# Global filter and gated feed-forward on one core: four PSUM banks and a new place for the filter copies in the first sequence

## The chip, the cores and the metric

The kernel runs on one core of one Trainium2 chip. The metric is the device time in microseconds (us) of one execution. The core has five engines that run their own instruction streams and meet at semaphores: PE (TensorE, matrix products into PSUM), DVE (VectorE), ACT (ScalarE), POOL (GpSimd) and SP (SyncE, which here only issues DMAs). POOL issues DMAs too.

## The reference

`x` is 8 sequences of 3008 tokens by 256 features. A filter acts in the frequency domain, and its output goes into a gated feed-forward block:

```python
X = np.fft.rfft(x, axis=1)
Y = X * (filt_r + 1j * filt_i)[None, :, :]
y = np.fft.irfft(Y, n=x.shape[1], axis=1).reshape(-1, 256)
rms = np.sqrt(np.mean(y * y, axis=-1, keepdims=True) + 1e-06)
xn = y / rms * rms_g
g = xn @ w_gate                       # 256 -> 1536
out = (g / (1 + exp(-g)) * (xn @ w_val)) @ w_out
```

## The kernel before

3008 is 47 x 64, so each transform is two small dense products with tables of sines and cosines, with a multiplication by the filter between the forward and the inverse one. The sequences are numbered `b` = 0 to 7. For `b` = 1 to 7 the mixing steps are laid by a plan (`at(slot, ...)`) between the feed-forward steps of the sequence before: one slot per block of 128 hidden features (`gv`, the gate and value products, and `down`, the output product), 576 slots in all. The instructions stand in the order in which the program writes them; no scheduler moves them.

Nothing can cover the mixing of sequence 0, so it stands alone ahead of slot 0. This first part is what the change touches. It keeps the data in SBUF, where later sequences go through HBM. In order of the program:

- **Set-up.** `x_load` (L180, eight DMAs on POOL's queue), clearing of half of each filter tile (POOL L613 and L614, DVE L620, ACT L610), and `f_load` (L464): real filters `fr[c]` on SP's queue, imaginary filters `fi[c]` on POOL's queue, for four chunks `c` of 8 frequencies. Behind the last `fi` chunk POOL issues `w_load(0)`, the first third of the three weight matrices.
- **Tables.** `wi_group(g)` (L556), g = 0 to 7, transposes a group of tables on PE into PSUM (`pst`); DVE copies one half out and ACT the other. Both halves take fixed PSUM banks, `bank(0)` and `bank(3)`. Groups 0 to 3 run ahead of `at_unit`, groups 4 to 7 between its calls. `warm_up(n)` (L575) is n products of zeros into a scratch bank.
- **Forward transform.** `at_unit(m, dh)` (L489) makes `aT`; one half is copied by DVE, the other by ACT. `at_unit` m reads columns 4m to 4m+3 of `x`, six columns to a chunk. `t1_unit(g)` (L501), g = 0 to 7, transposes `aT` (`pt`), in two PSUM banks that alternate; DVE copies the even ones and ACT the odd ones. `b_unit(0, i)` (L228), i = 0 to 15, is the second product (`psb`), two frequencies each, in four banks.
- **Filter.** Each filter tile is needed in both halves of the partitions. `f_dup(c)` (L475) copies 64 partitions to the other 64: chunk 0 by DVE (L478) and ACT (L485), the real part of chunks 1 and 2 by ACT (L480), all others by POOL (L482, L487). Calls stand ahead of i = 0, 3, 7 and 11. `b_unit` i uses chunk i/4. Its two products (L262, L263) run on DVE straight from PSUM, except for i = 1, 4, 7, 10, where ACT first copies the PSUM tile to `v` (L260) and POOL multiplies.
- **Inverse transform.** `bit_unit(i)` (L521) makes `pgt`, copied to `gT` (L538, L536) by ACT and once by DVE. Pairs of them stand behind `b_unit` i = 5, 7, ... with a lag of five, four behind the loop.
- **To the first feed-forward block.** `t2_unit` (L540) transposes `gT`. `n_first` (L361) is the last product, of which ACT takes the square `sq` and DVE the scaled `y`. `q_unit(0, 0)` sums the squares on PE (`psq`), DVE makes `u`, POOL takes the power -0.5 (`rho`, L347), `scale_split` halves it into two fp16 numbers `hl`, `warm_up(6)` follows, `scale_apply` spreads `hl` over the partitions on PE (`psr`), and DVE makes `xn`. Then slot 0 starts with `gv`.

`w_load(1)` and `w_load(2)` are issued by POOL behind `b_unit` i = 11. `bank(i)` (L192) names the six PSUM places that all these steps share: `mx`, `pg` (two buffers), `pv` (two buffers), `mb`, `po1`, `po0`.

Of the kernel before, what the change touches and what calls it, by code (L numbers as in the profile page):

```python
# [11 lines left out]
FP16 = mybir.dt.float16  # L12
AXT = mybir.ActivationFunctionType
ALU = mybir.AluOpType
# [6 lines left out]
P = 128  # L21
D = 256
# [7 lines left out]
HALF = 64  # L30
# [92 lines left out]
def kernel(  # L123
# [11 lines left out]
    nc = tc.nc  # L135
# [35 lines left out]
    gsb = glob.tile([P, 2], FP32)  # L171
# [20 lines left out]
    def bank(i, name):  # L192

        pool, tag = ((psM, "mx"), (psG, "pg"), (psV, "pv"), (psB, "mb"), (psO, "po1"), (psO, "po0"))[i]
        return pool.tile([P, 512], FP32, tag=tag, name=name)
# [32 lines left out]
    def b_unit(b, i):  # L228
        if b:
            ps = bank(3, "psb")  # L230
        else:
            ps = bank((0, 3, 4, 5)[i % 4], "psb")
        ps = ps.rearrange("p (a d) -> p a d", a=2)
        for u in range(2):
            k = 2 * i + u
            if b:
                w, t = late_p["wb"], st[b]["t2"][k // KC][:, k % KC, :]
            else:
                w, t = wbp, st[0]["t2"][k // 4][:, k % 4, :]
            nc.tensor.matmul(ps[:, u, :], w[:, k, :], t, start=True, stop=True)  # L240
        f1, f2 = filt(2 * i, 2)
        if b:
            s1 = late_p["sp"].tile([P, 2, D], FP16, tag="s1", name="s1")
            s2 = late_p["sp"].tile([P, 2, D], FP16, tag="s2", name="s2")
            if b > 1:
                nc.vector.tensor_tensor(out=s1, in0=ps, in1=f1, op=ALU.mult)  # L246
                st[b]["s"][i] = (s1, s2, ps, f2)
                return
        elif i % 2:
            s1 = hp.tile([P, 512], FP16, tag="sg", name="sg").rearrange("p (a d) -> p a d", a=2)  # L250
            s2 = hhs[(i // 2) % 4].rearrange("p (a d) -> p a d", a=2)
        else:
            ss = xnp.tile([P, 2, 512], FP16, tag="xn", name="ss")
            s1, s2 = (ss[:, e, :].rearrange("p (a d) -> p a d", a=2) for e in range(2))
        eng = nc.vector
        if (i % 3 == 1) if b else (i in (1, 4, 7, 10)):
            eng = nc.gpsimd
            v = yp.tile([P, 2, 512], FP32, tag="y", name="v")
            v = v[:, 0, :].rearrange("p (a d) -> p a d", a=2)
            nc.scalar.activation(out=v, in_=ps, func=AXT.Copy)  # L260
            ps = v
        eng.tensor_tensor(out=s1, in0=ps, in1=f1, op=ALU.mult)  # L262
        eng.tensor_tensor(out=s2, in0=ps, in1=f2, op=ALU.mult)  # L263
        st[b]["s"][i] = (s1, s2)
# [96 lines left out]
    def n_first():  # L361

        y = yp.tile([P, 2, 512], FP32, tag="y", name="y")
        sq = sqp.tile([P, 2, 512], FP16, tag="sq", name="sq")
        for dh in range(2):
            ps = bank(1 + dh, "psn")
            for q in range(4):
                nc.tensor.matmul(ps[:, ts(q, P)], st[0]["t4"][0][:, q, ds(dh * P, P)], wai2,
                                 start=True, stop=True)
            nc.scalar.activation(out=sq[:, dh, :], in_=ps, func=AXT.Square)  # L370
            nc.vector.tensor_scalar(out=y[:, dh, :], in0=ps, scalar1=gsb[:, dh:dh + 1], scalar2=None,
                                    op0=ALU.mult)
        st[0]["sq"][0] = sq
        st[0]["y"][0] = y

# [88 lines left out]
    def f_load(c, src, t, p0, eng):  # L464
        lo = 1 if c == 0 else 0
        eng.dma_start(t[p0 + 16:p0 + 63:2, :, :].rearrange("p a d -> p (a d)"),
                      raw(src, c * KC, [[64 * D, 24], [1, KC * D]]))
        for g in range(2):
            eng.dma_start(t[p0 + 1 + 24 * g:p0 + 24 + 24 * g:2, lo:KC, :],
                          raw(src, 64 * (1 + 11 * g) - c * KC - lo,  # L470
                              [[64 * D, 12], [-D, KC - lo], [1, D]]))
        if c == 0:
            eng.dma_start(t[p0 + 1:p0 + 48:2, 0, :], raw(src, 32, [[64 * D, 24], [1, D]]))

    def f_dup(c):  # L475
        a, e = fr[c][HALF:P], fr[c][0:HALF]
        if c == 0:
            nc.vector.tensor_copy(out=a, in_=e)  # L478
        elif c < 3:
            nc.scalar.activation(out=a, in_=e, func=AXT.Copy)  # L480
        else:
            nc.gpsimd.tensor_copy(out=a, in_=e)  # L482
        a, e = fi[c][0:HALF], fi[c][HALF:P]
        if c == 0:
            nc.scalar.activation(out=a, in_=e, func=AXT.Copy)  # L485
        else:
            nc.gpsimd.tensor_copy(out=a, in_=e)  # L487

    def at_unit(m, dh):  # L489
        ps = bank(1 + dh, "pat")  # L490
# [10 lines left out]
    def t1_unit(g):  # L501
        if g < 6:
            if g % 2 == 0:
                st[0]["t2t"] = t2p.tile([KR, KC, D], FP16, tag="t2", name="t2")
            dst = st[0]["t2t"][:, 4 * (g % 2):4 * (g % 2) + 4, :]
        else:
            dst = t3p.tile([KR, 4, D], FP16, tag="t3", name="t2")
        st[0]["t2"][g] = dst
        ps = psO.tile([P, 4, D], FP16, tag="po%d" % (g % 2), name="pt1")
        af = aT.rearrange("p a k -> p (a k)")  # L510
        for a in range(4):
            for dh in range(2):
                b0 = dh * H * P
                src = af[:, b0:b0 + 32 * P].rearrange("p (i k) -> p k i", k=K2)[:, 4 * g + a, :]
                nc.tensor.transpose(ps[:, a, ts(dh, P)], src, ident)
        if g % 2 == 0:
            nc.vector.tensor_copy(out=dst, in_=ps[0:KR])
        else:
            nc.scalar.activation(out=dst, in_=ps[0:KR], func=AXT.Copy)
# [36 lines left out]
    def wi_group(g):  # L556

        lo = 1 if g == 0 else 0
        for e in range(2):
            ps = bank(3 * e, "pst").rearrange("p (a d) -> p a d", a=4)  # L560
            for a in range(lo, 4):
                w = wbp[:, 4 * g + a, :]
                if e:
                    for p0 in (0, HALF):
                        nc.tensor.matmul(ps[p0:p0 + HALF, a, :], w[:, HALF - p0:P - p0], pm,
                                         start=True, stop=True)
                else:
                    nc.tensor.matmul(ps[:, a, :], w, pm, start=True, stop=True)
            dst = wi[:, e, 4 * g + lo:4 * g + 4, :]
            if e:  # L570
                nc.scalar.activation(out=dst, in_=ps[:, lo:4, :], func=AXT.Copy, scale=sgn)
            else:
                nc.vector.tensor_copy(out=dst, in_=ps[:, lo:4, :])

    def warm_up(n):  # L575
        pw = bank(4, "pw")
        for i in range(n):
            nc.tensor.matmul(pw, wz[:, 0:P], wz, start=True, stop=True)

# [5 lines left out]
    def w_load(q):  # L585
        cols = ts(q, DFF // 3)
        for src, dst in ((moe_w_gate, wg), (moe_w_val, wv)):
            nc.gpsimd.dma_start(dst[:, :, cols], src.rearrange("(dt p) j -> p dt j", p=P)[:, :, cols])
        nc.gpsimd.dma_start(wo[:, ts(q, JT // 3), :],
                            moe_w_out.rearrange("(jt p) d -> p jt d", p=P)[:, ts(q, JT // 3), :])  # L590

    with tc.manual_schedule():
# [28 lines left out]
            zero(fi[c][HALF:P])  # L621
        for c in range(4):
            f_load(c, filt_r, fr[c], 0, nc.sync)
            f_load(c, filt_i, fi[c], HALF, nc.gpsimd)
        w_load(0)
        with nc.allow_non_contiguous_dma(reason="one gain a partition"):
            nc.sync.dma_start(gsb, moe_rms_g.rearrange("(a p) -> p a", p=P))

        warm_up(16)
        for g in range(4):  # L630
            wi_group(g)
        warm_up(4)
        for m in range(6):
            for dh in range(2):
                at_unit(m, dh)
            if m < 4:
                wi_group(m + 4)
                warm_up(2)
        for i in range(8):
            t1_unit(i)  # L640
        f_dup(0)
        for i in range(16):
            if i % 4 == 3 and i < 15:
                f_dup(i // 4 + 1)
            b_unit(0, i)
            if i % 2 and i >= 5:
                bit_unit(i - 5)
                bit_unit(i - 4)
            if i == 11:
                w_load(1)  # L650
                w_load(2)
        for i in range(12, 16):
            bit_unit(i)
        t2_unit(0, 1)
        t2_unit(1, 0)
        n_first()
        t2_unit(2, 1)
        t2_unit(3, 0)
        q_unit(0, 0)
        t2_unit(4, 1)  # L660
        t2_unit(5, 0)
        scale_split(0)
        warm_up(6)
        scale_apply(0, 1)
        for c in range(NXC):
            x_load(1, c)
# [122 lines left out]
```

## Time and profile before

| | us |
|---|---|
| median of 15 runs | 952.79 (951.13 to 957.91) |
| profiled execution, its own time | 952.95 |
| its span, first to last instruction | 951.1 |

So 1.85 us of the profiled execution lie outside its span. Over the whole span PE is busy for 899.3 us (95%), DVE for 666.7 (70%), ACT for 632.5 (66%) and POOL for 391.6 (41%).

The first part, by stages of the span (busy us of each engine, PE's granted clock as a share of full speed):

| stage, us | what runs | PE | DVE | ACT | POOL | clock |
|---|---|---|---|---|---|---|
| 0 to 20.9 | tables, `at_unit` | 17.27 | 15.07 | 15.86 | 15.58 | 1.00 |
| 20.9 to 28.5 | `t1_unit` | 5.39 | 4.24 | 4.10 | 2.62 | 1.00 |

A busy time counts overlapped instructions once. In lines of the timeline, the first number is the start and the second the length in us, then come engine, line and operation, what is written and read, how many instructions are merged, and in brackets the idle time of the engine just before and what ended it.

### The profile page before, as it was taken

The page shows a single profiled execution, that of the slowest core. Times are in us where ns is not written, and L with a number is a line of the kernel's source. Part 1 is how long each engine was busy: PE and PEld are TensorE (multiplying, and loading weights), DVE is VectorE, ACT ScalarE, POOL GpSimd, SP SyncE. Part 2 cuts the span into 40 slices and gives each one's busy share as a digit, 9 for nine tenths or more (in the row PEclk, how much of TensorE's full clock was granted, in tenths as well). Part 3 has the DMA queues.
Part 4 walks back from the last instruction along what each step waited for, and adds up shares of the span by engine and source line. Part 5 has one row for each costly group of instructions (what it writes and reads, how often), then busy time and mean ns, then how long its engine had stood idle before and what let it go on. Part 6 is the DMA issues. An engine that isn't in the chain of part 4 may idle for free.

```text
span 951.1 us, 17799 instructions
## 1 busy us (share of the span) xinstructions
PE 899.3 (95%) x6339; PEld 565.0 (59%) x6339; DVE 666.7 (70%) x1051; ACT 632.5 (66%) x1066; POOL 391.6 (41%) x316
## 2 busy tenths in 40 slices
PE   8669788989999999999999999999999999999997
PEld 5546455555556666566666666666666666666654
DVE  6544445677778878788768788688868888555554
ACT  7647567577757776687757776687757775576543
POOL 7742269444532554145522554135522554033200
PEclk9779899999999999999999999999999999999999
DMA  9483655843466535743565435733353223322211
GB/s 200 75 132 82 173 117 112 208 101 85 109 138 131 122 74 103 182 101 90 117 147 125 123 73 109 178 80 79 98 143 94 78 64 65 108 62 57 52 27 45
DMA packets 87509, 101.21 MB, mean 106 GB/s; under 512 B 15984, under 2 KB 64048, under 8 KB 87036
## 3 DMA queue, kind: packets, MB, share of 16 engines
q1 hardware_dynamic: 78476, 83.82, 35.5%
q0 software_dynamic: 8944, 16.26, 10.9%
q8 instruction: 50, 0.82, 0.4%
q14 instruction: 39, 0.32, 0.1%
HBM read 67.93 MB, written 46.79 MB: 121 GB/s over the span
## 4 chain that ended last, share of the span: by engine, by line
PE 72%; DVE 8%; DMA 7%; POOL 5%; issue 4%; ACT 3%; SPq 0%; POOLq 0%; DVEq 0%; ACTq 0%
PE po L437 21%; PE pg L420 21%; PE pv L420 20%; DVE hh L425 3%; DMA t<-g_tmp 3%; PE psi L285 3%; PE psb L240 2%; PE psn L320 2%; PE psa L204 2%; DVE o L443 1%; ACT sg L424 1%; POOL s L276 1%; DMA g_tmp<-t 1%; DVE s L273 1%; DMA rb<-r_tmp 1%
## 5 line engine op out<-in xcount | busy, mean ns | idle before, releaser
L425 DVE TENSOR_TENSOR hh<-pv,sg 128x512 f16<-128x512 f32 (+1 forms) x576 | 391.9, 680 | 234.4 <-ACT sg L424 119.2
L424 ACT ACTIVATE sg<-pg 128x512 f16<-128x512 f32 (+1 forms) x576 | 338.9, 588 | 243.4 <-PE pg L420 235.4
L437 PE MATMUL po<-wo,hh 128*128 128x256 f16 x2256 | 344.0, 273 | 1.9
L420 PE MATMUL pg<-xn,wg 128*128 128x512 f16 (+1 forms) x1152 | 338.4, 375 | 1.0 <-DVE xn L393 1.0
L420 PE MATMUL pv<-xn,wv 128*128 128x512 f16 (+1 forms) x1152 | 338.4, 375 | 0.0
L437 PEld LDWEIGHTS <-hh 128*128 128x128 f16 x2256 | 216.6, 98 | 110.4 <-issue 11.2
L276 POOL TENSOR_TENSOR s<-s,s 128x512 f16<-128x512 f16 x96 | 110.7, 1153 | 352.9 <-DVE s L273 297.7
L420 PEld LDWEIGHTS <-wv 128*128 128x128 f16 x1152 | 112.7, 98 | 132.0 <-issue 1.6
L404 POOL TENSOR_TENSOR xn<-y,rb 128x1024 f16<-128x1024 f32 (+1 forms) x46 | 129.0, 2804 | 64.2 <-DMA rb<-r_tmp 56.9
L273 DVE TENSOR_TENSOR s<-psb,fi 64x512 f16<-64x512 f32 x192 | 132.3, 689 | 5.9
L420 PEld LDWEIGHTS <-wg 128*128 128x128 f16 x1152 | 109.1, 98 | 13.9 <-issue 1.7
L290 ACT ACTIVATE t<-psi 96x512 f16<-96x512 f32 x112 | 66.4, 593 | 20.8 <-PE psi L285 16.6
L347 POOL TENSOR_TENSOR rho<-u,mhalf 128x4 f32<-128x4 f32 (+1 forms) x48 | 48.5, 1011 | 64.0 <-DVE u L345 63.6
L326 ACT ACTIVATE y<-psn,gsb 128x512 f32<-128x512 f32 (+1 forms) x94 | 63.8, 679 | 9.9 <-PE psn L320 2.0
L246 DVE TENSOR_TENSOR s<-psb,fr 128x512 f16<-128x512 f32 x96 | 65.5, 682 | 4.1 <-PE psb L240 3.5
L206 ACT ACTIVATE t<-psa 128x512 f16<-128x512 f32 x84 | 50.2, 597 | 11.4 <-PE psa L204 7.9
L285 PE MATMUL psi<-s,wi 128*128 128x256 f16 x248 | 45.5, 272 | 10.7 <-POOL s L276 5.7
L332 ACT ACTIVATE sq<-psn 128x512 f16<-128x512 f32 (+1 forms) x94 | 54.7, 582 | 0.0
L240 PE MATMUL psb<-t,wb 96*128 96x256 f16 x224 | 43.1, 273 | 4.1 <-DMA t<-z_tmp 4.1
L285 PEld LDWEIGHTS <-wi 128*128 128x128 f16 x248 | 24.1, 97 | 38.4 <-issue 13.9
L320 PEld LDWEIGHTS <-t 128*128 128x128 f16 x368 | 28.4, 98 | 23.3 <-issue 3.1
L320 PE MATMUL psn<-tb,t 128*128 128x128 f16 x368 | 35.9, 219 | 2.4 <-ACT sq L332 1.0
(96 smaller groups left out, 482.5 us busy)
## 6 DMA issues: line engine op xcount, KB each, us to landing
out_dram<-o SPq DMA_DIRECT2D x84, 256.0 KB
xc<-in_x_dram POOLq DMA_DIRECT2D x56, 192.0 KB, 5.7
rb<-r_tmp SPq DMA_DIRECT2D x42, 256.0 KB
z_tmp<-t SPq DMA_DIRECT2D x112, 96.0 KB
t<-z_tmp SPq DMA_DIRECT2D x28, 384.0 KB
g_tmp<-t SPq DMA_DIRECT2D x56, 192.0 KB
t<-g_tmp SPq DMA_DIRECT2D x92, 96.0 KB
out_dram<-o SPq DMA_DIRECT2D x12, 192.0 KB
```

Of the source, the lines that this page charges most:

```text
L246: nc.vector.tensor_tensor(out=s1, in0=ps, in1=f1, op=ALU.mult)
L273: nc.vector.tensor_tensor(out=s2[a], in0=ps[e], in1=f2[e], op=ALU.mult)
L276: nc.gpsimd.tensor_tensor(out=s, in0=s1, in1=s2, op=ALU.add)
L285: nc.tensor.matmul(ps[:, u, :], wi_at(q, 2 * i + u), ss[q][:, u, :], start=(q == 0), stop=(q == n - 1))
L290: nc.scalar.activation(out=st[b]["t3"][c][:, 2 * r:2 * r + 2, :], in_=ps[0:KR], func=AXT.Copy)
L320: nc.tensor.matmul(ps[:, ts(q, P)], st[b]["t4"][n1p // XC][:, n1p % XC, ds(dh * P, P)], wai if b else wai2, start=True, stop=True)
L326: nc.scalar.activation(out=y[:, dh, 0:w], in_=ps[:, 0:w], func=AXT.Identity, scale=gsb[:, dh:dh + 1])
L404: nc.gpsimd.tensor_tensor(out=xv, in0=yv, in1=rv.unsqueeze(1).to_broadcast([P, 2, n, P]), op=ALU.mult)
L420: nc.tensor.matmul(ps[:, 0:w], wt[:, dt_, ts(jt, P)], xn[:, dt_, 0:w], start=(dt_ == 0), stop=(dt_ == 1))
L424: nc.scalar.activation(out=sg[:, 0:w], in_=pg[:, 0:w], func=AXT.Silu)
L425: nc.vector.tensor_tensor(out=hh[:, 0:w], in0=pv[:, 0:w], in1=sg[:, 0:w], op=ALU.mult)
L437: nc.tensor.matmul(po[s4 // 2][:, s4 % 2, :], hh[:, ts(s4, P)], wo[:, jt, :], start=(jt == 0 and s4 % 2 == 0), stop=(jt == JT - 1 and (s4 ...
```

## The change

Four things change, all of them in the first part:

1. `wi_group` and `t1_unit` each take four PSUM banks in turn instead of two. The copy of `t1_unit` 7 goes from ACT to DVE. Groups 4 and 5 stand together behind `at_unit` 0, groups 6 and 7 behind 1 and 2. The calls of `warm_up` there are left out but the first, which has 14 products instead of 16.
2. `f_dup` copies chunks 0 and 1 on POOL, chunk 2 on ACT, and of chunk 3 the real part on ACT and the imaginary part on POOL. On POOL's queue the copies of chunk 0 now stand behind the DMAs of `fi` chunk 2, then the DMAs of `fi` chunk 3, then the copies of chunk 1, then `w_load(0)`. The copies of chunk 2 stand ahead of `b_unit` i = 4, those of chunk 3 ahead of i = 9.
3. The four products that POOL makes are those of i = 2, 5, 8, 11 instead of 1, 4, 7, 10.
4. In `n_first` ACT makes the first half of `y`, behind both squares. The six warm-up products ahead of `psr` become two behind the first two `t2_unit`, three behind the next two, and four ahead of `scale_split`, all in bank `mx`.

```diff
-        if (i % 3 == 1) if b else (i in (1, 4, 7, 10)):
+        if (i % 3 == 1) if b else (i in (2, 5, 8, 11)):
...
-            nc.vector.tensor_scalar(out=y[:, dh, :], in0=ps, scalar1=gsb[:, dh:dh + 1], scalar2=None,
-                                    op0=ALU.mult)
+            if dh:
+                nc.vector.tensor_scalar(out=y[:, dh, :], in0=ps, scalar1=gsb[:, dh:dh + 1], scalar2=None,
+                                        op0=ALU.mult)
+            else:
+                y0, p0 = y[:, dh, :], ps
+        nc.scalar.activation(out=y0, in_=p0, func=AXT.Identity, scale=gsb[:, 0:1])
...
     def f_dup(c):
-        a, e = fr[c][HALF:P], fr[c][0:HALF]
-        if c == 0:
-            nc.vector.tensor_copy(out=a, in_=e)
-        elif c < 3:
-            nc.scalar.activation(out=a, in_=e, func=AXT.Copy)
-        else:
-            nc.gpsimd.tensor_copy(out=a, in_=e)
-        a, e = fi[c][0:HALF], fi[c][HALF:P]
-        if c == 0:
-            nc.scalar.activation(out=a, in_=e, func=AXT.Copy)
-        else:
-            nc.gpsimd.tensor_copy(out=a, in_=e)
+        for t, a, e in ((fr[c], HALF, 0), (fi[c], 0, HALF)):
+            if c == 2 or (c == 3 and a):
+                nc.scalar.activation(out=t[a:a + HALF], in_=t[e:e + HALF], func=AXT.Copy)
+            else:
+                nc.gpsimd.tensor_copy(out=t[a:a + HALF], in_=t[e:e + HALF])
...
-        ps = psO.tile([P, 4, D], FP16, tag="po%d" % (g % 2), name="pt1")
+        pool, tag = ((psO, "po0"), (psO, "po1"), (psM, "mx"), (psB, "mb"))[g % 4]
+        ps = pool.tile([P, 4, D], FP16, tag=tag, name="pt1")
...
-        if g % 2 == 0:
+        if g % 2 == 0 or g == 7:
...
-            ps = bank(3 * e, "pst").rearrange("p (a d) -> p a d", a=4)
+            ps = bank((0, 3, 4, 5)[(2 * g + e) % 4], "pst").rearrange("p (a d) -> p a d", a=4)
...
-    def warm_up(n):
-        pw = bank(4, "pw")
+    def warm_up(n, bk):
+        pw = bank(bk, "pw")
...
             f_load(c, filt_r, fr[c], 0, nc.sync)
-            f_load(c, filt_i, fi[c], HALF, nc.gpsimd)
-        w_load(0)
+            if c < 3:
+                f_load(c, filt_i, fi[c], HALF, nc.gpsimd)
...
-        warm_up(16)
+        warm_up(14, 1)
         for g in range(4):
             wi_group(g)
-        warm_up(4)
         for m in range(6):
             for dh in range(2):
                 at_unit(m, dh)
-            if m < 4:
-                wi_group(m + 4)
-                warm_up(2)
+            for g in ((4, 5), (6,), (7,), (), (), ())[m]:
+                wi_group(g)
         for i in range(8):
             t1_unit(i)
         f_dup(0)
+        f_load(3, filt_i, fi[3], HALF, nc.gpsimd)
+        f_dup(1)
+        w_load(0)
         for i in range(16):
-            if i % 4 == 3 and i < 15:
-                f_dup(i // 4 + 1)
+            if i == 4:
+                f_dup(2)
+            if i == 9:
+                f_dup(3)
             b_unit(0, i)
...
         t2_unit(1, 0)
+        warm_up(2, 0)
         n_first()
         t2_unit(2, 1)
         t2_unit(3, 0)
+        warm_up(3, 0)
         q_unit(0, 0)
         t2_unit(4, 1)
         t2_unit(5, 0)
+        warm_up(4, 0)
         scale_split(0)
-        warm_up(6)
         scale_apply(0, 1)
```

## The prediction

> **What bounds the kernel now.** First the table of stages:
>
> ```profile
> 28.50:54.40 25.90, 16.35 (x157) 12.75 (x156) 15.04 (x25) 14.35 (x22) 21.81 (x18) 0.67 0.37 56
> 54.40:65.80 11.40, 8.48 (x56) 5.56 (x57) 4.44 (x11) 2.88 (x5) 5.52 (x10) 0.56 0.94 141
> 120.00:951.00 831.00, 805.27 (x5583) 504.00 (x5580) 603.92 (x947) 560.30 (x956) 332.10 (x241) 1.00 0.44 103
> ```
>
> (Columns: stage, length, busy PE, PE weight loads, DVE, ACT, POOL, clock, DMA.) From 120 us on PE is busy 97%, and the change leaves that part alone. All of the change lies ahead of 65.8 us. There PE waits for others, and in the filter stage POOL is the busiest (84%). Next the chain of waits, from 45 us to the first complete gate product at 65.79:
>
> ```profile
> 45.04 1.86 POOL fr L482
> ...
> 46.96 1.90 POOL fi L487
> ...
> 49.50 0.68 DVE sg L262
> ...
> 54.39 1.22 PE pt L549 x8
> ...
> 57.34 1.41 DVE y L371 x2
> ...
> 60.84 2.72 PE pw L578 x6
> 63.56 0.87 PE psr L389 x8
> ```
>
> POOL's last two copies end last; DVE then makes its remaining seven products, 0.60 us apart, to 53.18; PE and ACT finish `gT` by 54.34. The rest is a row of short steps, one of them six warm-up products at half clock (0.453 us each). DVE's timeline says who is late, and POOL's why:
>
> ```profile
> 46.94 0.69 DVE L262 TENSOR_TENSOR ss<-psb,fr 128x512 f16<-128x512 f32 x1 [3.89 <-POOL fr L482]
> 48.89 0.69 DVE L263 TENSOR_TENSOR ss<-psb,fi 128x512 f16<-128x512 f32 x1 [1.26 <-POOL fi L487]
> ```
>
> ```profile
> 25.12 0.76 POOL L589 DMA_DIRECT2D wo<-in_moe_w_out_dram  x1 [0.42 <-DMA fi<-in_filt_i_dram]
> 30.95 1.27 POOL L262 TENSOR_TENSOR sg<-v,fr 128x512 f16<-128x512 f32 x1 [5.07 <-ACT v L260]
> 32.19 1.26 POOL L263 TENSOR_TENSOR hh<-v,fi 128x512 f16<-128x512 f32 x1
> 33.52 1.89 POOL L487 COPY fi<-fi 64x2048 f32<-64x2048 f32 x1
> ```
>
> POOL waits 5.07 us until 30.95 and then works without a gap to 48.85: four pairs of products (2.5 us each) and four copies (1.89 each). In `t1_unit` the wait is for banks, as PE's timeline shows:
>
> ```profile
> 24.96 1.19 PE L515 MATMUL pt<-tb,aT 128*128 128x128 f16 x16 [0.50 <-ACT t L519]
> 26.73 0.67 PE L515 MATMUL pt<-tb,aT 128*128 128x128 f16 x8 [0.58 <-ACT t L519]
> ```
>
> **The banks.** Today table groups come 1.16 us apart, each half waiting for its bank. With four banks DVE's copies follow at 0.60, so group 3 is copied at 10.5 instead of 12.2, and a warm-up of 0.97 us goes. Ten copies (four tables, six `aT`) by 0.60 to 0.69 on each of DVE and ACT then run to about 17.2. The last chunk of `x` lands at 15.24 by the trace's landing records, which leaves this nearly as it is. `aT` is complete at 17.25 instead of 20.87. The eight `t1_unit` take 0.66 us of PE each, with no wait for a bank (bank 0 is read by 18.8 and needed at 20.1). PE is done at 22.7 and DVE's last two copies at 23.4, instead of 28.45: **5.0 us earlier**. This alone is no gain; what counts is who is last behind it.
>
> **POOL's new row.** Landing records: `fr` chunk 0 at 18.40, `fi` 0 at 19.04, `fr` 1 at 22.89, `fi` 1 at 23.68, `fr` 2 at 28.98, `fi` 2 at 26.28, `fi` 3 at 29.33, `fr` 3 at 31.95. POOL has issued `fi` 2 by 18.3. Then two copies to 22.3, three DMA issues (0.55 + 0.6 + 0.6) to 24.1, two copies to 27.9, three weight issues (0.76 + 0.72 + 0.76) to 30.2. Moving `fi` 3 past two copies costs nothing: its issue ends at 24.1 while the queue is busy with `fi` 2 until 26.28, and it is read only at 38.5. `w_load(0)` is issued 4.3 to 6.4 us later and landed 9 us after its issue today; slot 0 needs it at 55. The pair of i = 2 runs from 30.2 to 32.7. The pair of i = 5 needs `v` from ACT, which now sits behind the copies of chunk 2: ACT waits for `fr` 2 from 24.4 to 28.98 and then copies to 32.8 (1.91 each), `v` at 33.4. So i = 5 runs to 35.95, i = 8 to 38.5, the copy of `fi` 3 to **40.4**, i = 11 to 42.9. Queued behind ACT's two copies are `gT` copies and the next `v`; PE has two buffers for `pgt`, and `v` of i = 8 is made at 35.9, when POOL wants it.
>
> DVE makes i = 0, 1, 3 (23.4 to 27.0), waits for `fi` 1 (27.9), makes 4, 6, 7 to 31.0, and 9 and 10 by 38.4. The first product of i = 12 is made by 39.9, the second waits for 40.4, and seven products by 0.60 end at **44.6 instead of 53.18**: 8.5 us. POOL's last pair, 42.9, is done by then; PE has four pairs left of 0.35 us at full clock or 0.65 at half. DVE loses a copy (1.22) and a `y` (0.7).
>
> POOL's copies read while DVE reads PSUM. POOL's product takes 1.27 us beside DVE in the rows above, so I add nothing for sharing.
>
> **The tail.** From the last product to `pt` 1.21 us as today: 45.8. At half clock, with today's durations: eight `pt` 1.22, two warm-ups 0.91 (beside ACT's copy 0.6, so 0.3 on the path), `psn` 0.85, `pt` 0.85, three warm-ups 1.36, `psq` 0.35, `u` 0.2, `rho` 1.05 and `hl` 0.4 (beside them `pt` and four warm-ups, 2.65, which end last by 0.95), `psr` 0.9, `xn` 1.3: the first complete gate product at 56.25, 9.5 us earlier than 65.79. At full clock the warm-ups hide, and `sq`, `u`, `rho` and `hl` are the path: 52.7, 13.1 us earlier. The row of this stage says 0.56 of full speed, so I lie nearer the half-clock end: 10.5. `y` on ACT behind both squares ends ahead of `psr` in both sums.
>
> Sum: 952.95 - 10.5 = 942.45; against the median (0.16 lower) **942.3**. Behind slot 0 everything shifts together: weights 2 and 3 are issued from 42.9, landed 11 us after the first issue today, and slot 4 needs them at 60.
>
> **Two rules weighed.** The program has a library reload for POOL right ahead of its first product, in both kernels. The Trainium skill (GPSIMD Engine Reference, Instruction dispatch) says that the first call of a freshly loaded routine pays about 6 us for code, with no instruction to be seen. The row: POOL's 5.07 us idle ends 0.09 after `v`, so a cost of up to 5 could be hidden there, and 6 could not. Today's 5 us cover is gone in the new order (`v` is made at 25). The row gives 0 to 5.07, the rule 6. I take 0, since copies and products in the same row follow each other without a gap. The other: TensorE: Matmul & The Clock Gate (The HAM clock gate) states that PE's clock halves after idle windows and needs some 3.4 us of steady work to come back. The row: half clock from 50.8 to 64.45, full just as slot 0 starts, behind 3.6 us of unbroken warm-ups and `psr`. The new warm-ups are spread; by the rule slot 0 may start at half clock. PE is only 75% busy in the first 10 us of slots, so one window of 3.4 us there costs 1 us or so. By the row I add nothing, by the rule 1 us; it stays in the range.
>
> **Rivals.** (1) The reload is exposed: POOL is 5.1 to 6 us later, less 0.75 that i = 5 waits anyway; the products end at 49 to 49.8, and with the shorter tail the time is 947 to 948. Chance 0.17. (2) The denser row keeps PE at full clock in the tail: 939 to 940. For it, the new row has 2 us less idle between bursts; against it, waits for POOL at 30 and 40 us. 0.13. (3) **Slower**: slot 0 starts at half clock and stays there. A PE-bound slot loses half its time, so the 10.5 us are eaten from 21 us of half clock on; at 25 us the time is 955. Against it, the chip raised the clock after one full window wherever the trace is dense, and the slots are. 0.05. (4) The change does nothing, because landings set the pace: `fr` 2 at 28.98 is late for ACT. The sum has this wait and it costs 0.75; if landings moved by 8 us it would be true, within 0.2% of before. 0.03. The forecast itself, 940 to 945: 0.62.
>
> The 80% range is 938.3 to 948, from full clock to an exposed reload. About 0.2% (2 us) is what can be told from no change: faster 0.93, same 0.02, slower 0.05.
>
> **What would show it.** Right: `t1_unit` without waits for banks, done near 23.4; POOL's copies from 18.5; POOL's first product near 30.2; DVE's last near 44.6; the first complete gate product at 53 to 56. A gap on POOL between the third weight issue and its first product is the reload. The forecast is wrong if POOL's copies are stretched well over 1.9 us, or if the gain at the first gate product is not found at the end.

## The result and the profile after

| | before | changed |
|---|---|---|
| median, us | 953.26 (949.92 to 957.91, 47 runs) | 939.88 (939.06 to 943.28, 9 runs) |
| profiled execution, us | 952.95 | 943.11 |
| its span, us | 951.1 | 941.3 |

The ratio of the times is 0.9866, 95% interval [0.9851, 0.9881]: the changed kernel is 12.8 us faster (11.3 to 14.2). The forecast was 942.3, a gain of 10.5.

The stages of the changed kernel, cut where the same steps end (`t1_unit` copied, `gT` complete, first complete gate product; the columns are those of the stage table in the prediction):

```profile
25.90:46.00 20.10, 12.58 (x158) 10.00 (x158) 15.14 (x26) 13.94 (x22) 19.76 (x19) 0.87 0.54 83
46.00:55.00 9.00, 7.85 (x58) 5.17 (x59) 3.89 (x10) 3.34 (x6) 4.68 (x8) 0.72 1.16 168
110.00:941.00 831.00, 805.00 (x5568) 503.36 (x5565) 602.08 (x945) 558.61 (x954) 331.62 (x240) 1.00 0.44 102
```

Up to the end of `t1_unit` 2.5 us are gone. The filter stage is 20.1 us long instead of 25.9, and POOL is busy in 98% of it: it is still who is last, with nothing left between its instructions. The tail is 9.0 us instead of 11.4. The last row is as dense as before (805.00 us of 831, before 805.27), so in this pair of executions the gain lies ahead of slot 0. The end of the same stretch in the chain of waits (start, length in us, what):

```profile
39.16 1.17 POOL fi L484
...
40.41 1.26 POOL sg L262
41.67 1.23 POOL hh L263
...
46.00 1.20 PE pt L547 x8
47.20 0.85 PE pw L576 x2
48.06 0.85 PE psn L368 x8
48.91 0.85 PE pt L547 x8
49.77 1.28 PE pw L576 x3
51.05 0.20 PE psq L341 x8
...
55.04 0.38 PE pg L424
```

POOL again leads, through the copy of `fi` 3 and the pair of i = 11. The first complete gate product starts at 55.04 instead of 65.79: 10.75 us earlier, against 10.5 in the forecast. Both the spread warm-ups that do lie on the path are seen, the two (0.2 us longer than ACT's copy beside them) and the three (1.28 us). POOL's timeline says what the library reload cost:

```profile
26.75 1.89 POOL L484 COPY fi<-fi 64x2048 f32<-64x2048 f32 x1
28.58 0.77 POOL L586 DMA_DIRECT2D wg<-in_moe_w_gate_dram  x1
29.34 0.74 POOL L586 DMA_DIRECT2D wv<-in_moe_w_val_dram  x1
30.06 0.78 POOL L587 DMA_DIRECT2D wo<-in_moe_w_out_dram  x1
30.98 1.26 POOL L262 TENSOR_TENSOR ss<-v,fr 128x512 f16<-128x512 f32 x1
32.21 1.25 POOL L263 TENSOR_TENSOR ss<-v,fi 128x512 f16<-128x512 f32 x1
```

The third weight issue ends at 30.84 and the first product starts at 30.98. The reload's two records (`MODIFY_POOL_CONFIG`, at 30.81 and 30.85) lie there, so it cost 0.14 us at most. Why it cost so little the trace does not say.

### The profile page after: what moved, and what is told of

It is laid out like the page before. It is cut to its first block, busy times and chain, and to the rows that moved or that the text cites. A ratio compares the mean times of both kernels' runs of the same rounds, so it can differ in the third digit from the quotient of the medians.

```text
span 941.3 us, 17781 instructions
## 1 busy us (share of the span) xinstructions
PE 894.4 (95%) x6328; PEld 562.5 (60%) x6328; DVE 664.7 (71%) x1050; ACT 630.7 (67%) x1066; POOL 392.9 (42%) x317
## 3 DMA queue, kind: packets, MB, share of 16 engines
q0 software_dynamic: 8944, 16.26, 11.1%
## 4 chain that ended last, share of the span: by engine, by line
PE 75%; DVE 7%; DMA 6%; POOL 5%; issue 4%; ACT 3%; SPq 0%; POOLq 0%; DVEq 0%; ACTq 0%
PE po L441 22%; PE pg L424 22%; PE pv L424 21%; DVE hh L429 3%; PE psi L285 3%; PE psb L240 2%; PE psn L320 2%; PE psa L204 2%; DMA t<-z_tmp 1%; POOL s L276 1%; DVE o L447 1%; DVE s L273 1%; ACT sg L428 1%; DMA z_tmp<-t 1%; POOL xn L408 1%
## 5 line engine op out<-in xcount | busy, mean ns | idle before, releaser
L285 PE MATMUL psi<-s,wi 128*128 128x256 f16 x248 | 45.8, 274 | 11.9 <-POOL s L276 5.6
L320 PEld LDWEIGHTS <-t 128*128 128x128 f16 x368 | 28.5, 98 | 22.3 <-issue 1.9
```

Source lines behind the costliest of these rows:

```text
L285: nc.tensor.matmul(ps[:, u, :], wi_at(q, 2 * i + u), ss[q][:, u, :], start=(q == 0), stop=(q == n - 1))
L320: nc.tensor.matmul(ps[:, ts(q, P)], st[b]["t4"][n1p // XC][:, n1p % XC, ds(dh * P, P)], wai if b else wai2, start=True, stop=True)
```

## Experiments

The marks below are from the one profiled execution of each kernel; the times and ratios are from all its runs, against runs of before on the same chip. "Forward" is the end of the copies of `t1_unit`, "POOL" the start of its first product, "products" the end of DVE's last one, "slot 0" the start of ACT's first gate activation.

| kernel | forward | POOL | products | slot 0 | median, us | ratio [95%] |
|---|---|---|---|---|---|---|
| before | 28.45 | 30.95 | 53.17 | 66.20 | 953.26 | |
| changed | 25.93 | 30.98 | 44.64 | 55.45 | 939.88 | 0.9866 [0.9851, 0.9881] |
| banks alone | 26.23 | 27.96 | 50.14 | 63.18 | 946.62 | 0.9928 [0.9909, 0.9947] |
| copies alone | 29.91 | 31.13 | 46.62 | 60.06 | 945.44 | 0.9911 [0.9892, 0.9930] |
| tail alone | 28.45 | 30.95 | 53.15 | 63.24 | 950.16 | 0.9967 [0.9954, 0.9980] |
| changed, old banks | 28.42 | 31.05 | 45.12 | 55.38 | 941.99 | 0.9874 [0.9854, 0.9894] |
| changed, again | 25.78 | 30.76 | 44.43 | 54.28 | 940.59 | 0.9850 [0.9829, 0.9871] |
| before, again (one run) | 28.44 | 30.94 | 53.13 | 66.02 | 950.99 | |
| no warm-ups in the tail | 24.09 | 31.21 | 45.21 | 55.83 | 942.08 | 0.9869 [0.9847, 0.9890] |
| late weights | 23.28 | 28.49 | 42.50 | 51.68 | 938.28 | 0.9832 [0.9812, 0.9853] |
| before, filled | 29.88 | 32.38 | 54.58 | 67.55 | 951.17 | 0.9986 [0.9974, 0.9997] |
| changed, filled | 25.70 | 31.81 | 45.82 | 55.00 | 940.87 | 0.9862 [0.9841, 0.9884] |
| late weights, filled | 28.43 | 29.86 | 45.35 | 55.48 | 936.52 | 0.9829 [0.9805, 0.9853] |

**Banks alone.** The kernel before with part 1:

```diff
-        ps = psO.tile([P, 4, D], FP16, tag="po%d" % (g % 2), name="pt1")
+        pool, tag = ((psO, "po0"), (psO, "po1"), (psM, "mx"), (psB, "mb"))[g % 4]
+        ps = pool.tile([P, 4, D], FP16, tag=tag, name="pt1")
...
-            ps = bank(3 * e, "pst").rearrange("p (a d) -> p a d", a=4)
+            ps = bank((0, 3, 4, 5)[(2 * g + e) % 4], "pst").rearrange("p (a d) -> p a d", a=4)
...
```

> The kernel before with part 1 alone (four banks, order of the groups, warm-ups there). Theory A (GpSimd's row of copies and products is who is last; the banks are only cover): GpSimd's first product moves from 30.95 to about 27.8, because ScalarE is free of its transposes some 3 us earlier, and the row behind it keeps its length: 3 us faster than before, ratio 0.997. Theory B (each part carries its own share and the shares add): 4 to 5 us faster, and copies alone and tail alone bring the rest.

In the profile the marks are those of theory A: POOL's first product at 27.96, slot 0 3.0 us earlier. But the time fell by 6.9 us (5.1 to 8.7), more than either theory said. This profiled execution, 948.62 us, was the slowest of the six, and of the 4.3 us that its span is shorter than that of before, 1.3 lie behind slot 0. In it `x` came late and TensorE's clock fell at 17.0, so that the transposes ended at 26.2; in the kernel with late weights, without that half-clock window, they ended at 23.28. With the old place of the copies POOL starts when the transposes are done, so 2.9 us more could be had in the other five executions. That fits, but those have no trace: it is argued, not shown. Whether the parts add is told by the next runs.

**Copies alone.** The kernel before with parts 2 and 3:

```diff
+        for t, a, e in ((fr[c], HALF, 0), (fi[c], 0, HALF)):
+            if c == 2 or (c == 3 and a):
+                nc.scalar.activation(out=t[a:a + HALF], in_=t[e:e + HALF], func=AXT.Copy)
+            else:
+                nc.gpsimd.tensor_copy(out=t[a:a + HALF], in_=t[e:e + HALF])
...
         f_dup(0)
+        f_load(3, filt_i, fi[3], HALF, nc.gpsimd)
+        f_dup(1)
+        w_load(0)
...
```

> The kernel before with parts 2 and 3 alone (filter copies, order on GpSimd's queue, late products). Theory A: VectorE's last product at about 44.6 instead of 53.2 although the transposes still end at 28.4; 8.5 us faster than before, ratio 0.991. Theory B: what banks and tail leave of the 13 us, 5 to 6 us, ratio 0.994.

8.5 us faster (6.7 to 10.3), the number of theory A, but in part by luck: slot 0 is only 6.1 us earlier, and the span of this execution 7.0 us shorter. The products ended at 46.6, not 44.6. POOL's timeline of this kernel:

```profile
31.13 1.27 POOL L262 TENSOR_TENSOR ss<-v,fr 128x512 f16<-128x512 f32 x1 [0.34 <-ACT v L260]
32.36 1.26 POOL L263 TENSOR_TENSOR ss<-v,fi 128x512 f16<-128x512 f32 x1
35.40 1.27 POOL L262 TENSOR_TENSOR sg<-v,fr 128x512 f16<-128x512 f32 x1 [1.78 <-ACT v L260]
```

ACT's own transpose copies run to 29.9 here, the two filter copies and `v` follow, and POOL waits 1.78 us for the `v` of i = 5. The transposes ended 1.5 us later than before, with the clock at half from 11.1 to 14.5; the filled kernel before, further down, has the same stretch and the same end. So the banks are not all cover: through ACT a late end of the transposes can cost up to 2 us.

**Tail alone.** The kernel before with part 4:

```diff
-            nc.vector.tensor_scalar(out=y[:, dh, :], in0=ps, scalar1=gsb[:, dh:dh + 1], scalar2=None,
-                                    op0=ALU.mult)
+            if dh:
+                nc.vector.tensor_scalar(out=y[:, dh, :], in0=ps, scalar1=gsb[:, dh:dh + 1], scalar2=None,
+                                        op0=ALU.mult)
...
-        warm_up(6)
...
```

> The kernel before with part 4 alone (y on ScalarE, warm-ups spread). Both theories: the way from the last product to the first complete gate product falls from 12.6 to about 10.5, so 2 us faster, ratio 0.998. If the spread warm-ups leave slot 0 at half clock: 1 us less than that.

3.1 us (1.9 to 4.4); slot 0 is 2.96 us earlier with the products where they were. A little more than expected, and slot 0 did start at full clock: in this execution the half-clock window ended at 57.7 instead of 64.45.

**Changed, old banks.** The same edit as the first, in reverse, on the changed kernel.

> The changed kernel with part 1 undone. Theory A: transposes end at 28.4 instead of 25.9, but GpSimd's row starts from the landings, VectorE's last product stays at 44.6, and the time stays within 1 us of the changed kernel: about 13 us faster than before, ratio 0.987. Theory B: 4 to 5 us of the gain go, ratio 0.991.

Theory A: 12.0 us (10.1 to 13.9) of the 12.8 stay, the products end 0.5 us later, and slot 0 is where it was. So on top of copies and tail the banks bring nothing that can be told. By the times the three parts alone sum to 18.5 us and together bring 12.8: banks and copies both bring forward the same thing, the end of POOL's row (48.85 before, 45.83 with the banks alone, 44.87 with the copies alone, 42.90 with all). The traces say the same at the end of DVE's products: alone the banks bring 3.0 us there, but on top of the other parts 0.5. It is less there than by the times, though. At slot 0 the three alone sum to 12.1 us, and all together bring 10.75 in one trace and 11.9 in the other. The times of the banks alone and of the copies alone go beyond that by 3.9 and 2.4 us, and this is not explained.

**Both kernels again**, unchanged, for a second profiled execution.

> The changed kernel once more, for a second profiled execution and more runs. Theory A (the whole gain is made ahead of slot 0, and the profiled execution of before lost 3 us by a half-clock window at 126 to 129.5): the first gate product again 10 to 11 us earlier than 65.8, and without such a window a span near 938.3. Theory C (the stage of slots 28 to 40 is slower in the changed kernel whatever the clock): the same 2 to 3 us lost there again.

> The kernel before once more, one look, for a second profiled execution. Theory A: the first complete gate product again at 65 to 67 us; what differs from the first profile is where half-clock windows fall behind slot 0, up to 3 us.

Theory A in both. Slot 0 at 54.28 and 66.02, 11.7 us apart. The window at 126 did not come again: from slot 32 to slot 40 this execution of the changed kernel took 17.4 us, the first one 21.2. Its span is 939.0, not 938.3: another window, at 112.4, cost 1.7 us between slots 28 and 32. So each execution loses to such windows in other places. Both pairs keep a little less at the end than at slot 0: 9.8 us of 10.75, and 10.2 of 11.7. The clock is not all of it. From slot 32 to slot 34 TensorE also waits for POOL's products of sequence 1 in some executions, 1.8 us in the first of the changed kernel and none in the second.

**No warm-ups in the tail.**

```diff
-        warm_up(2, 0)
...
-        warm_up(3, 0)
...
-        warm_up(4, 0)
```

> The changed kernel without its nine warm-up products behind the filter stage. By the sum: the sums of squares start 1.3 us earlier (the three products ahead of them took 1.28 us), the first gate product 1 to 1.5 us earlier. By the rule of the clock: TensorE is then less busy from 46 to 53, slot 0 starts at half clock, and 1 to 2 us go there again: within 1 us of the changed kernel, either side.

942.08 against 940.59 on the same chip, 1.5 us slower; the intervals overlap. From the last product to `u` it took 5.9 us, against 6.6 and 5.7 in the two traces of the changed kernel, so the gain of the plain sum is not seen. The clock is at half from 50.6 to 57.4, so `psr` and the first slots run at half speed, and slot 0 starts no earlier. The trace thus sides with the clock against the plain sum of durations; that the warm-ups pay in time is likely, but not settled by ratios that overlap.

**Late weights.** The row of POOL in the changed kernel has three weight issues, 2.26 us, in the middle of its path. This version moves them behind the last pair:

```diff
         f_dup(1)
-        w_load(0)
...
             if i == 11:
+                w_load(0)
                 w_load(1)
                 w_load(2)
```

> The changed kernel with the first third of the weights issued behind GpSimd's last pair of products instead of ahead of its first. Theory A: GpSimd's row starts at 28.7 instead of 31.0 and its last copy ends near 38.5 instead of 40.4, VectorE's last product near 42.7, 1.9 us faster than the changed kernel; the weights land near 48 to 49 and are needed at 52.8. If ScalarE (the copies of v) is who is last: no gain. If the weights come too late: slower.

938.28 us, 2.3 us below the changed kernel on the same chip (1.7% below before). The intervals of the two overlap, but slot 0 is 2.6 us earlier than in the changed kernel's trace on that chip. Products at 42.50 against 42.7 expected. Its POOL row:

```profile
26.51 1.89 POOL L484 COPY fi<-fi 64x2048 f32<-64x2048 f32 x1
28.49 1.27 POOL L262 TENSOR_TENSOR ss<-v,fr 128x512 f16<-128x512 f32 x1
...
36.30 1.89 POOL L484 COPY fi<-fi 64x2048 f32<-64x2048 f32 x1
38.27 1.27 POOL L262 TENSOR_TENSOR sg<-v,fr 128x512 f16<-128x512 f32 x1
```

**Filled wait.** 13 products whose result is not read, into the bank that `b_unit` takes next, ahead of the first `b_unit` of sequence 1, in the kernel before, the changed one and the one with late weights:

```diff
+    def fill(n):
+        pw = bank(3, "pw")
+        for i in range(n):
+            nc.tensor.matmul(pw, wg[:, 0, 0:P], wg[:, 0, 0:512], start=True, stop=True)
...
+            if b == 1:
+                at(b_at[0], fill, 13)
             for i in range(16):
```

> The kernel before with 13 unused products (2.8 us at full clock) ahead of the first b_unit of sequence 1, where TensorE waits 3 us for z_tmp and the clock then falls. Theory D (half-clock windows behind slot 0 make the part of the gain that the first part does not show): no window between slots 24 and 36, 2 to 3 us faster than before, ratio 0.9975. Theory E (those windows lie where others are waited for): within 0.5 us of before, or slower by what the 13 products overrun the wait.

> The changed kernel with the same 13 products. Theory D: it loses less to windows already (clock 0.99 against 0.98), so 1 to 2 us faster than the changed kernel, and the distance between the two filled kernels falls from 13 us to the 11 us of the first part. Theory E: as the changed kernel, 0.986.

> The kernel with the late weights and the same 13 products: Theory D 1 to 2 us below the 938.3 without them; Theory E 938.3.

The kernel before gains 1.3 us (0.3 to 2.5), less than theory D said. The changed one and the one with late weights gain nothing that can be told (0.9862 and 0.9829 against 0.9866 and 0.9832), but with intervals 4 to 5 us wide a gain of 1 us could not be told either. The filling does what it should: 2.97 us of products take the place of the wait, of which 0.26 to 0.34 are left, and in the changed kernel no half-clock window falls behind slot 0 until the last microsecond. In the filled kernel before one still does, at 123.6, and in the one with late weights one at 112.1.

In the traces the stretch from slot 24 to slot 34 takes 28.8 to 29.4 us filled and 29.7 to 31.9 in the ten others. In the filled changed kernel 2.1 us of it are a wait for POOL, without any fall of the clock. PE's timeline there, then POOL's:

```profile
123.20 0.27 PE L285 MATMUL psi<-s,wi 128*128 128x256 f16 x1 [1.13 <-POOL s L262]
124.42 0.49 PE L285 MATMUL psi<-s,wi 128*128 128x256 f16 x3 [0.95 <-POOL s L263]
```

```profile
113.46 2.85 POOL L408 TENSOR_TENSOR xn<-y,rb 128x1024 f16<-128x1024 f32 x1 [5.80 <-DMA rb<-r_tmp]
116.42 5.39 POOL L268 TENSOR_SCALAR fi<-fi 64x2048 f32<-64x2048 f32 x1
121.89 1.26 POOL L262 TENSOR_TENSOR s<-v,fr 128x512 f16<-128x512 f32 x1
```

POOL starts on a landing and then changes the sign of half a filter chunk (L268), 5.39 us, ahead of the products that TensorE needs. So what is won ahead of this place can be lost to POOL again, as theory E has it. Theory D holds in sign for the kernel before; for the changed kernel the two are not decided.

## Why the prediction was right, and where its size was off

The direction, the range and the mechanism were right. The median itself, 939.88, lies just outside the 940 to 945 of the forecast, among the 939 to 940 of rival (2), although both traces of the changed kernel show half the clock at the start of the tail.

**POOL sets the end: right.** First product 30.98 (forecast 30.2), last copy ended at 40.33 (40.4), last pair at 42.9 (42.9), DVE's last product at 44.64 (44.6). Two misses inside cancelled, which is luck. POOL began 0.8 us late: the last chunk of `x` landed at 16.59 and not at 15.24, POOL's issues of `fi` 2 waited for it and ended at 18.95, and `fr` 0 came 0.3 us after that. The 15.24 was the earliest of all 13 profiled executions (the latest is 17.07), so one trace was a poor base for it. And `fr` 2 landed at 26.9 instead of 28.98, so the 0.75 us wait for `v` never came: it had rested on the old landing, taken over although the copies leave a gap in POOL's DMAs.

**Banks as cover: right for this kernel,** shown by the run with old banks (0.9874 against 0.9866). The figure for the forward transform itself was wrong: 25.9 instead of 23.4. With full clock, in the kernels with late weights and without the tail's warm-ups, the transposes ended 7.0 us after the last chunk of `x` (16.24 to 23.28, 17.07 to 24.09); here it was 9.3. So 2.3 us are the clock's, which fell to half at 16.87. The late `x` is 1.35 us, and the working itself was 1.1 us too long (15.24 and 7.0 make 22.3). In the changed kernel this cost nothing that can be seen, since POOL was later.

**Tail: right.** From the last product to the first complete gate product it took 10.4 us. The working has 8.1 at full clock and 11.65 at half, but a slip is in the latter: its terms sum to 55.5 us and not to 56.25, which makes it 10.9. The clock was half until 51.0, as the row of the kernel before suggested. In the second execution it rose at 47.5, and the way took 9.4; in the filled changed kernel and the one with late weights, at full clock throughout, 8.8.

**Library reload: the row was the better guide.** At most 0.14 us, where the rule would have had 6.

**Where the forecast was short by 2.3 us.** The mis-sized term is the gain at slot 0, worked out from one execution of before. Up to slot 0 the filled kernels are the same as the ones without filling, so three traces of each kernel show this part. Slot 0 starts at 66.20, 66.02 and 67.55 before and at 55.45, 54.28 and 55.00 changed: 11.7 us apart in the mean, 10.6 to 13.3 by pairs. The forecast had 10.5, and the profiled pair 10.75. With 11.7 the interval of the result (11.3 to 14.2) is met.

The remaining microsecond is not seen behind slot 0. "Everything shifts together" failed there in the other direction: from slot 0 to the end the two traces of before take 884.9 and 883.2 us, those of the changed kernel 885.9 and 884.7, for the waits and windows named above. What the traces lack is more executions. The profiled one of the changed kernel was a long one for this kernel: its granted clock was 0.986, the median of its nine runs is 0.990, and among these nine a run is 0.5 us longer for each 0.001 less of clock (correlation -0.95), which makes some 2 of the 3.2 us between it and the median. Before has a median clock of 0.980 (58 runs, made along with the experiments). Over such spans 0.980 and 0.990 are some 38 and 19 us at half clock. Ahead of slot 0 the traces of the two kernels without filling show 24 to 27 and 14 to 17 us of it; the other half of the distance shows in none of them.

One cause can be named that one pair of traces does not show: half-clock stretches at the very start. In the filled kernel before, one at 11 us delayed the whole first part by 1.35 us. The kernel with late weights is not safe from them, although its POOL row also starts from landings: in its filled version the clock was at half from 9.7 to 23.4, POOL then waited 1.68 and 1.77 us for `v`, and slot 0 came at 55.48 instead of 51.68. For the changed kernel itself no trace has such a stretch. How often they come is not known, and the rest stays open.

## What to carry to other kernels

Before several waits are removed at once, ask which engine's row ends last with all of them gone: here the banks alone gave 7 us, but nothing that can be told on top of the other parts (12.0 and 12.8), because the engine that ends last no longer waited for what they make faster. An issue of a DMA took POOL's time like a computation (0.75 us for each of the weights here), and on the engine that ends last it belongs behind the work that others wait for. Where the clock falls differently from run to run, look at the clocks of all runs, and at more than one trace of each kernel, before a gain is read: by pairs of traces it was 10.6 to 13.3 us here.

## What the runs showed of the hardware

TensorE's clock halved behind short gaps. In all 13 traces the half-clock stretches ahead of the end are 3.41 us long or a multiple of it. TensorE's busy time in windows of that length which end where the clock changed or could have (columns: window, length, busy with the number of products, clock, DMA share, GB/s), first in the changed kernel:

```profile
13.46:16.87 3.41, 1.58 (x29) 1.00 0.95 182
27.10:30.52 3.42, 1.98 (x24) 1.00 0.84 141
30.52:33.93 3.41, 0.63 (x11) 1.00 1.14 166
```

and in the kernel before:

```profile
23.49:26.90 3.41, 2.33 (x33) 1.00 1.03 184
26.90:30.32 3.42, 1.53 (x16) 1.00 1.05 218
33.73:37.14 3.41, 3.41 (x32) 0.50 0.00 0
```

The clock halved at 16.87, 33.93 and 30.32, behind windows with 46%, 18% and 45% of busy time, and stayed behind windows with 58% and 68%. It rose at 37.14 behind a window that was busy throughout. At 16.87 the longest idle stretch had been 1.83 us, TensorE's wait for a chunk of `x`. The Trainium skill (TensorE: Matmul & The Clock Gate, HAM oscillation) warns of gaps over 3.4 us; here a gap of half that length sufficed.

Nor does the busy share alone decide. With the same windows laid over all 13 traces, each of the 43 at full clock with 45% busy or less was followed by half clock, and none with over 75%. Between the two both happened: 23 halved and 155 did not. The first row below is from the kernel with late weights, and the clock stayed; the second is from the one without the tail's warm-ups, with no gap over 0.31 us, and it halved:

```profile
190.18:193.59 3.41, 1.57 (x13) 1.00 0.00 0
47.20:50.62 3.42, 2.53 (x32) 1.00 1.27 184
```

Rival (3) of the prediction takes one full window to bring the clock back; it did not always. In the filled kernel with late weights it stayed at half behind three in a row:

```profile
9.73:13.14 3.41, 3.41 (x39) 0.50 1.11 231
13.14:16.55 3.41, 3.41 (x38) 0.50 0.95 227
16.55:19.97 3.42, 3.42 (x38) 0.50 0.87 213
```

The products of `at_unit` show that this is no slip of the record: eight of them took 1.03 us there, and 0.62 in the kernel with late weights at full clock. What else the clock goes by is not shown. The clock columns of the stage tables count time without a clock record as full. Before's first 6.4 us are such time, and its warm-up products stand 0.427 us apart in it, against 0.217 right behind it, so that it too was at half.
